# Sliding-window attention and a two-layer network on one core: score blocks of 64 queries by 128 keys, row sums from ones beside the values, chunks of 256 queries

## The chip, the cores and the metric

The kernel runs on one core of a Trainium2 chip. The metric is the time of one launch on the device in microseconds (us). The core has engines with a queue of instructions each, executed in the queue's order: PE multiplies matrices (PEld is its loading of weights), DVE and POOL work on vectors, ACT applies functions and copies, SP issues most of the transfers (DMA). PE writes to PSUM, which has eight banks; POOL does not read PSUM in this kernel.

## What is computed

For batch 8, 8 heads, 576 positions and head size 64 the reference does this (shortened):

```python
scores = scale * np.matmul(q, k.transpose(0, 1, 3, 2))
mask = np.abs(pos[:, None] - pos[None, :]) <= 32
scores = np.where(mask, scores, -1000000000.0)
attn = np.exp(scores - np.max(scores, axis=-1, keepdims=True))
attn = attn / (np.sum(attn, axis=-1, keepdims=True) + 1e-09)
x = np.matmul(attn, v)                  # heads side by side: 4608 tokens x 512
h = x @ w_in                            # 512 x 2048
out = np.maximum(0.01 * h, h) @ w_out   # 2048 x 512
```

A query meets at most 65 keys, those up to 32 positions away.

## The kernel before

**Units.** Attention is cut into units of one pair of heads (four pairs, one on partitions 0 to 63 and one on 64 to 127 of each tile) and one half of a batch's 576 queries, 288 of them: 64 units. `score` (L270) multiplies blocks of 64 keys with the queries that can reach them. The keys of a pair lie in `kbd` as blocks of 128 by 128 with one head in each diagonal quarter and zeros elsewhere, so one matmul does both heads. Five matmuls of 128, 128, 128, 96 and 64 columns make a unit's scores in the PSUM tile `ps`. ACT takes the exponential (L280, 576 columns), POOL multiplies with the mask (L282, `prob`). `product` (L312) multiplies `prob` with the values `vbd`, which are laid out in diagonal quarters too, in five matmuls. `sums` (L295) gets the row sums, broadcast to 64 partitions each, with a matmul by a block-diagonal matrix of ones (L301 on the two halves of `prob` that DVE has added in `join`, L292, from unit 12 on; L304 twice without that). DVE takes the reciprocal of the sums out of PSUM (L309) and multiplies (L334, `scaled`) into `xT`, the transposed input of the network.

**Network.** `h_tile` and `h_first` (L360, L369) make the first layer for one half of a batch, 288 tokens: 16 tiles `f` of four matmuls over the contraction (L348), each evicted by ACT with the leaky function (L355) into `gT`. `h_first` goes over the contraction outermost for four tiles, so that pass `c` needs only the units of pair `c`. `o_tile` (L381) makes 128 tokens of output by 16 matmuls of 512 columns (L390); ACT copies them out (L395, four buffers `o_sb`) and SP writes them. Four PSUM banks (`mm`) serve both layers.

**Inputs.** `load_qk` and `load_v` (L68, L87) fetch f32 data through SP's queue. POOL, and in the opening DVE and ACT, cast them to bf16 (L195, L197, L203, L205). Queries and keys of the first two batches are transposed on PE (`transposes`, L218) and copied out by ACT; later batches are transposed by a DMA (`transpose_dma`, L207). DVE copies the keys into the quarters of `kbd` (`place_keys`, L258, L260). From batch 2 on a packet of q or k has 512 bytes, as two rows go to one partition together.

**Order.** The program order is written by hand and every engine follows it. Lines 454 to 568 are the opening: batch 0 and its first layer, with `keep_busy` (L398), 21 matmuls whose result nobody uses, between them. POOL issues the loads of the weights (L448, L452), and a one-element memset on POOL (L75) holds back the loads of batch 1. In the opening a cast of batch 1 on DVE stands one or two pairs ahead of its transposes (`second_pair`, L546). From L574 a plan lists the network's work with its costs, and `spend` (L595) calls `step` (L420) whenever a unit is due: it issues `score(i + 2)`, then unit i's sums, product and scaling, then the casts, transposes and loads due at that step. Units for one half batch are due evenly over the network's work on the half before, and end 4 us ahead of it (`LEAD`).

Of the kernel before, what the change touches and what calls it, by code (L numbers as in the profile page):

```python
# [16 lines left out]
def kernel(  # L17
# [13 lines left out]

    nc = tc.nc
# [8 lines left out]
    NB = S // 64  # L41
    HALF = S // 2
    DMC = DMODEL // 128
    FFC = DFF // 128
    EVEN = HALF // 2
# [5 lines left out]
    cast = ctx.enter_context(tc.tile_pool(name="cast", bufs=1))  # L51
    attn = ctx.enter_context(tc.tile_pool(name="attn", bufs=2))
    kt = ctx.enter_context(tc.tile_pool(name="kt", bufs=4))
    joined = ctx.enter_context(tc.tile_pool(name="joined", bufs=2))
    recip = ctx.enter_context(tc.tile_pool(name="recip", bufs=3))
    outp = ctx.enter_context(tc.tile_pool(name="outp", bufs=4))
    PS = bass.MemoryType.PSUM
    mmps = ctx.enter_context(tc.tile_pool(name="mmps", bufs=4, space=PS))
    scps = ctx.enter_context(tc.tile_pool(name="scps", bufs=1, space=PS))
    xps = ctx.enter_context(tc.tile_pool(name="xps", bufs=1, space=PS))  # L60


    qf, kf, vf = {}, {}, {}
    RUN = S // 96

    BY_DMA = 2

    def load_qk(b, p, behind=None):  # L68

        for into, src, name in ((qf, q, "qf"), (kf, k, "kf")):
            t = fload.tile([96, 2, RUN * D], FP32, name=f"{name}{p}")
# [3 lines left out]
            heads = src[b, 2 * p:2 * p + 2]  # L77
            if b < BY_DMA:
                nc.sync.dma_start(out=t, in_=heads.rearrange("a (p c) d -> p a (c d)", c=RUN))
            else:  # L80
                nc.sync.dma_start(
                    out=t.rearrange("p a (g e) -> p a g e", g=3),
                    in_=heads.rearrange("a (g p c) d -> p a g (c d)", g=3, c=2),
                )
            into[b, p] = t

    def load_v(b, p):  # L87

        t = fload.tile([128, NB, D], FP32, name=f"vf{p}")
        for a in range(2):  # L90
            nc.sync.dma_start(
                out=t[64 * a:64 * a + 64],
                in_=v[b, 2 * p + a].rearrange("(c p) d -> p c d", p=64),
            )
        vf[b, p] = t

    load_qk(0, 0)
    load_qk(0, 1)
    load_v(0, 0)
    load_qk(0, 2)  # L100
    load_qk(0, 3)
    for p in range(1, NPAIR):
        load_v(0, p)

# [6 lines left out]
    ones_bd = const.tile([128, 128], BF16)  # L111
    nc.vector.memset(ones_bd, 0.0)
    nc.vector.memset(ones_bd[0:64, 0:64], 1.0)
    nc.vector.memset(ones_bd[64:128, 64:128], 1.0)

# [3 lines left out]

    kbd = [const.tile([128, NPAIR, NB, 128], BF16, name=f"kbd{i}") for i in range(2)]  # L120
    vbd = [const.tile([128, NPAIR, NB, 128], BF16, name=f"vbd{i}") for i in range(2)]
    zero = const.tile([128, 1], BF16)
    nc.vector.memset(zero, 0.0)

    def clear(t, p):
        flat = t[:, p].rearrange("p n j -> p (n j)")
        nc.scalar.activation(
            out=flat, in_=zero.to_broadcast([128, NB * 128]), func=AF.Copy,
        )

    mask = [const.tile([128, 2, 2, EVEN], BF16, name=f"mask{i}") for i in range(2)]
    nc.vector.memset(mask[0][:, 1, :, 0:16], 0.0)
    nc.vector.memset(mask[1][:, 1, :, 128:EVEN], 0.0)
    nc.vector.memset(kbd[0], 0.0)  # L134
    clear(vbd[0], 0)
    clear(vbd[0], 1)
    clear(vbd[0], 2)

    WIN = [
        [((0, 0, 48), (2, 48, 64), (4, 112, 32)), ((1, 16, 64), (3, 80, 64))],
        [((4, 0, 32), (6, 32, 64), (8, 96, 48)), ((5, 0, 64), (7, 64, 64))],
    ]

    win = const.tile([128, 2, 3, 64], BF16)
    nc.gpsimd.memset(win, 1.0)
    for lo in (0, 64):
        w = win[lo:lo + 64]
        nc.gpsimd.affine_select(  # L150
            out=w, in_=w, compare_op=ALU.is_ge, fill=0.0,
            base=0, channel_multiplier=-1, pattern=[[1, 2], [0, 3], [2, 64]],
        )
        nc.gpsimd.affine_select(
            out=w, in_=w, compare_op=ALU.is_ge, fill=0.0,
            base=2 * W, channel_multiplier=1, pattern=[[-1, 2], [0, 3], [-2, 64]],
        )
    nc.gpsimd.memset(vbd[0][:, 3], 0.0)
    win_f = win.rearrange("p c m i -> p c (m i)")

    def make_mask(hf):
        lo = (16, 32)[hf]
        nc.gpsimd.tensor_copy(out=mask[hf][:, 0], in_=win_f[:, :, lo:lo + EVEN])
        lo = (16, 0)[hf]
        nc.gpsimd.tensor_copy(out=mask[hf][:, 1, :, lo:lo + 128], in_=win_f[:, :, 0:128])

    NPROB = 6
    prob = const.tile([128, NPROB, 2, 2, EVEN], BF16)

    ps = scps.tile([128, 1024], FP32)  # L170
    P0 = 512 - HALF
    ps_v = ps[:, P0:P0 + 2 * HALF].rearrange("p (n c i) -> p n c i", n=2, c=2)
    nc.scalar.activation(
        out=ps[:, 512:512 + HALF], in_=zero.to_broadcast([128, HALF]), func=AF.Copy,
    )


    RING = 4 * HALF
    xT = const.tile([128, NPAIR, RING], BF16)
    w_in_bf = const.tile([128, DMC, DFF], BF16)  # L180
    w_out_bf = const.tile([128, FFC, DMODEL], BF16)


    qT = {}

    def cast_qk(b, p, q_eng=None):
        for eng, src, dst in ((q_eng or nc.gpsimd, qf, qb), (nc.gpsimd, kf, kb)):
            if b < BY_DMA:
                parts = [(dst[:, p], src[b, p].rearrange("p a (c d) -> p c a d", d=D))]
            else:  # L190
                by_c = src[b, p].rearrange("p a (g c d) -> c p g a d", g=3, c=2)
                parts = [(dst[:, p, 3 * c:3 * c + 3], by_c[c]) for c in range(2)]
            for to, tok in parts:
                if eng is nc.scalar:
                    eng.activation(out=to, in_=tok, func=AF.Copy)  # L195
                else:
                    eng.tensor_copy(out=to, in_=tok)  # L197

    def cast_v(b, p, on_act=False, heads=range(2)):
        for a in heads:  # L200
            r = slice(64 * a, 64 * a + 64)
            if on_act:
                nc.scalar.activation(out=vbd[b % 2][r, p, :, r], in_=vf[b, p][r], func=AF.Copy)  # L203
            else:
                nc.gpsimd.tensor_copy(out=vbd[b % 2][r, p, :, r], in_=vf[b, p][r])  # L205

    def transpose_dma(b, p):  # L207
        if b not in qT:
            qT[b] = attn.tile([128, NPAIR, S], BF16, name="qT")
        kT = kt.tile([128, S], BF16, name="kT")  # L210
        for t, src in ((qT[b][:, p], qb), (kT, kb)):
            nc.sync.dma_start_transpose(
                out=t.rearrange("p (c i) -> p c i", c=RUN),
                in_=src[:, p].rearrange("p c a d -> p (c a d)"),
            )
        landing.append((8 * (b - 1) + 4 + p, b, p, kT))

    def transposes(b):  # L218

        qT[b] = attn.tile([128, NPAIR, S], BF16, name="qT")  # L220
        for p in range(NPAIR):
            for which, src in (("q", qb), ("k", kb)):
                tp = mmps.tile([128, RUN, 96], BF16, name="tp", tag="mm")
                for c in range(RUN):
                    nc.tensor.transpose(  # L225
                        tp[:, c],
                        src[:, p, c].rearrange("p a d -> p (a d)"),
                        ident[0:96, 0:96],
                    )

                tok = tp.rearrange("p (e c) i -> p c i e", c=2)
                if which == "q":
                    nc.scalar.activation(
                        out=qT[b][:, p].rearrange("p (c i e) -> p c i e", c=2, e=RUN // 2),
                        in_=tok, func=AF.Copy,
                    )
                else:
                    kT = kt.tile([128, S], BF16, name="kT")
                    nc.scalar.activation(  # L239
                        out=kT.rearrange("p (i c) -> p i c", c=RUN),  # L240
                        in_=tp.rearrange("p c i -> p i c"), func=AF.Copy,
                    )
                    unplaced.append((b, p, kT))
                yield

    unplaced, landing = [], []

    def place_keys():

        while landing and landing[0][0] <= state["done"]:  # L250
            unplaced.append(landing.pop(0)[1:])
        while unplaced:
            b, p, kT = unplaced.pop(0)
            for a in range(2):
                r = slice(64 * a, 64 * a + 64)
# [394 lines left out]
```

## Time and profile before

| what | value |
|---|---|
| median of 3 runs | 320.66 us (320.07 to 321.24) |
| profiled execution, first to last instruction (span) | 319.0 us |
| what the median has beyond the span | 1.66 us |
| busy: PE, DVE, POOL, ACT | 301.1, 220.7, 191.2, 183.5 us |
| instructions: PE, DVE, POOL, ACT | 2429, 258, 251, 394 |
| granted PE clock | 1.00 throughout |
| DMA | 108,400 packets, 49.46 MB, queue of SP 66.0% of 16 engines |
| last matmul's end | 315.9 us |

For the profiled execution nothing but its span is known; its own launch time is taken to be the span and 1.66 us around it. A group line of the profile names line, engine, operation and tiles, then shapes and count; after the bar stand busy time and the mean length of one in ns, then the engine's idle time just before them and what ended it. Matmuls overlap, so a matmul's mean length is more than what it adds: that is read from the distance between starts.

### The profile page before, as it was taken

To read this page: it belongs to the slowest core of one execution; us is meant where nothing else is said; L and a number is where in the kernel's file an instruction comes from. 1 tells how busy PE (TensorE), PEld (TensorE's weight loads), DVE (VectorE), ACT (ScalarE), POOL (GpSimd) and SP (SyncE) were. 2 spreads that over 40 slices of the span, in tenths; PEclk is the share of its full clock that TensorE was granted. 3 is DMA by queue.
4 is the path that set the end of the run, shared out by engine and by line. 5 is a ranking of instruction groups with operands and counts; after the bars stand their busy time and mean duration, and the time that the engine had idled before them with its cause. 6 is when DMAs were issued, how large, how long until landed. Compare 5 with 4: busy or idle time off the path is not lost.

```text
span 319.0 us, 6455 instructions
## 1 busy us (share of the span) xinstructions
PE 301.1 (94%) x2429; PEld 203.5 (64%) x2449; DVE 220.7 (69%) x258; ACT 183.5 (58%) x394; POOL 191.2 (60%) x251
## 2 busy tenths in 40 slices
PE   2678998999999999999999999999999999999996
PEld 1457764576765858576765858576665858576653
DVE  5688886869755987688755987688745988565100
ACT  7686688574652828375552828465552837464531
POOL 7899963974646866585646866586637866330000
PEclk9999999999999999999999999999999999999999
DMA  8999998997998989399835996399833440000102
GB/s 189 224 184 229 269 242 188 242 200 180 223 245 167 245 148 210 79 237 202 173 76 114 233 229 151 74 215 223 178 76 104 108 71 33 35 35 2 66 31 71
DMA packets 108400, 49.46 MB, mean 155 GB/s; under 512 B 68816, under 2 KB 103888, under 8 KB 108368
## 3 DMA queue, kind: packets, MB, share of 16 engines
q1 hardware_dynamic: 104144, 44.84, 66.0%
q0 software_dynamic: 4224, 4.19, 8.1%
q8 instruction: 19, 0.31, 0.5%
q14 instruction: 13, 0.11, 0.1%
HBM read 36.70 MB, written 9.44 MB: 145 GB/s over the span
## 4 chain that ended last, share of the span: by engine, by line
PE 88%; DVE 5%; ACT 3%; issue 2%; POOL 1%; ACTq 0%; POOLq 0%; DVEq 0%
PE mm L390 38%; PE mm L348 37%; PE x L320 5%; PE ps L275 5%; PE s L301 2%; DVE r L309 2%; DVE qb L197 1%; PE s L304 1%; DVE kbd L258 1%; POOL prob L282 1%; ACT kT L239 1%; PE tp L225 1%; ACT e L280 1%; ACT vbd L203 1%; DVE kbd L134 1%
## 5 line engine op out<-in xcount | busy, mean ns | idle before, releaser
L309 DVE RECIPROCAL r<-s 128x288 f32<-128x288 f32 x64 | 125.2, 1956 | 57.0 <-PE s L301 53.3
L282 POOL TENSOR_TENSOR prob<-e,mask 128x576 bf16<-128x576 bf16 x64 | 81.6, 1276 | 89.2 <-ACT e L280 42.1
L348 PE MATMUL mm<-xT,w_in_bf 128*128 128x288 bf16 x1024 | 134.0, 286 | 0.1
L390 PE MATMUL mm<-w_out_bf,gT 128*128 128x512 bf16 (+2 forms) x572 | 128.7, 373 | 1.1
L355 ACT ACTIVATE gT<-mm 128x288 bf16<-128x288 f32 x256 | 101.2, 412 | 25.6 <-PE mm L348 9.1
L348 PEld LDWEIGHTS <-w_in_bf 128*128 128x128 bf16 x1024 | 98.4, 98 | 24.5 <-issue 0.3
L390 PEld LDWEIGHTS <-gT 128*128 128x128 bf16 x592 | 56.3, 98 | 59.2
L395 ACT ACTIVATE o_sb<-mm 128x512 f32<-128x512 f32 (+2 forms) x37 | 21.7, 585 | 91.8 <-PE mm L390 89.0
L280 ACT ACTIVATE e<-ps 128x576 bf16<-128x576 f32 x64 | 41.5, 648 | 10.6 <-PE ps L275 10.5
L197 POOL CAST kb<-kf 96x384 bf16<-96x384 f32 (+1 forms) x56 | 34.8, 643 | 4.5 <-DMA kf<-in_k_dram 4.3
L205 POOL CAST vbd<-vf 64x576 bf16<-64x576 f32 x50 | 34.7, 694 | 1.5
L334 DVE TENSOR_TENSOR xT<-x,r 128x288 bf16<-128x288 f32 x64 | 29.2, 457 | 7.8 <-PE x L320 1.1
L260 DVE COPY kbd<-kT 64x576 bf16<-64x576 bf16 x48 | 32.3, 674 | 0.6 <-DMA kT<-kb 0.3
L320 PE MATMUL x<-prob,vbd 128*128 128x128 bf16 (+2 forms) x320 | 26.0, 213 | 2.7 <-ACT vbd L203 1.3
L275 PEld LDWEIGHTS <-kbd 128*128 128x128 bf16 x320 | 20.8, 99 | 10.7 <-DVE kbd L258 1.6
L275 PE MATMUL ps<-qT,kbd 128*128 128x128 bf16 (+2 forms) x320 | 26.3, 214 | 1.3 <-DVE kbd L258 0.8
L197 POOL CAST qb<-qf 96x384 bf16<-96x384 f32 x48 | 24.4, 536 | 0.0
L320 PEld LDWEIGHTS <-vbd 128*128 128x128 bf16 x320 | 20.5, 99 | 5.4 <-ACT vbd L203 1.9
L292 DVE TENSOR_TENSOR both<-prob 128x288 bf16<-128x288 bf16 x52 | 20.0, 384 | 0.9
L301 PE MATMUL s<-both,ones_bd 128*128 128x288 bf16 x52 | 14.9, 286 | 0.0
L258 DVE COPY kbd<-kT 64x576 bf16<-64x576 bf16 x16 | 7.1, 446 | 6.2 <-ACT kT L239 6.0
L225 PE MATMUL tp<-ident,qb 96*128 96x96 bf16 x48 | 4.1, 233 | 6.8 <-DVE qb L197 6.8
(43 smaller groups left out, 87.9 us busy)
## 6 DMA issues: line engine op xcount, KB each, us to landing
qf<-in_q_dram SPq DMA_DIRECT2D x32, 288.0 KB, 4.6
kf<-in_k_dram SPq DMA_DIRECT2D x32, 288.0 KB, 5.3
vf<-in_v_dram SPq DMA_DIRECT2D x64, 144.0 KB, 4.4
out_dram<-o_sb SPq DMA_DIRECT2D x35, 256.0 KB, 3.9
w_in_bf<-in_moe_w_in_dram POOLq DMA_DIRECT2D x4, 512.0 KB, 8.2
w_out_bf<-in_moe_w_out_dram POOLq DMA_DIRECT2D x4, 512.0 KB, 16.4
qT<-qb SPq DMA_TRANSPOSE x24, 4.2
kT<-kb SPq DMA_TRANSPOSE x24, 3.1
```

The source lines that it names most:

```text
L197: eng.tensor_copy(out=to, in_=tok)
L205: nc.gpsimd.tensor_copy(out=vbd[b % 2][r, p, :, r], in_=vf[b, p][r])
L260: nc.vector.tensor_copy(out=to.rearrange("p n (m c) -> p n c m", c=2), in_=kT[r].rearrange("p (c n m) -> p n c m", c=2, n=NB),)
L275: nc.tensor.matmul(ps_v[:, n_, :, i0:i0 + n], kbd[b % 2][:, p, blk], by_c[:, :, hf * EVEN + i0:hf * EVEN + i0 + n], start=True, stop=True,)
L280: nc.scalar.activation(out=e, in_=ps[:, P0:P0 + 2 * HALF], func=AF.Exp, scale=scale)
L282: nc.gpsimd.tensor_mul(pr.rearrange("p n c i -> p (n c i)"), e, mask[hf].rearrange("p n c i -> p (n c i)"),)
L309: nc.vector.reciprocal(r, s)
L320: nc.tensor.matmul(x_v[:, :, i0:i0 + n], vbd[b % 2][:, p, blk, :], pr[:, n_, :, i0:i0 + n], start=(blk == parts[0][1]), stop=(blk == parts ...
L334: nc.vector.tensor_mul(place(i), x, r)
L348: nc.tensor.matmul(h[:, 0:HALF], w_in_bf[:, c, ts(f, 128)], xT[:, c, ds(g * HALF % RING, HALF)], start=(c == 0), stop=(c == DMC - 1),)
L355: nc.scalar.activation(out=gT[:, f, ds(g * HALF % RING, HALF)].rearrange("p (i c) -> p i c", c=2), in_=h[:, 0:HALF].rearrange("p (c i) -> ...
L390: nc.tensor.matmul(o[:, lo:hi], gT[:, f, ds(128 * j % RING, 128)], w_out_bf[:, f, lo:hi], start=(f == 0), stop=(f == FFC - 1),)
```

## The change

The work is tiled anew. A unit is one pair of heads and 256 queries, counted through the 4608 tokens without regard to batches: 18 chunks, 72 units. A unit has four windows of 64 queries, and each window meets 128 keys, from 32 before to 32 behind. The keys lie plainly in `kz` with 32 zero columns at either end; the queries in `qz` are padded, each head with zeros in the other head's 64 partitions. One matmul of 128 columns does a window's scores for both heads. The values lie in `vw` as head 0, ones, head 1, so that a 128-wide weight holds one head's values and ones, and each product brings its row sums on the other 64 partitions: eight matmuls of 64 columns a unit. ACT then copies the sums across to the value's partitions (two copies of 64 by 256), DVE takes the reciprocal from SBUF and multiplies twice on 64 partitions.

The first layer takes 256 tokens for the first four chunks and 512 from then on. `sums`, `join`, `keep_busy`, `kbd` and `place_keys` go; the DMA transposes the keys straight into `kz`, and DVE copies the transposed queries into `qz` (`place_queries`, two contiguous copies per pair). PSUM has two banks for scores and two for `x`, which the opening's transposes share; before, `ps` was one tile over two banks, and `x` and `s` had one bank each. Output buffers go from four to three. One row goes to a partition in loads of q and k from batch 2 on, so packets have 256 bytes. The values are loaded in blocks of 128 rows shifted by 32.

```diff
+    CH = 256
     def score(i):
+        ps = scps.tile([128, 2, CH // 64, 64], FP32, name="ps")
+        for w, (b, m) in enumerate(windows(i)):
+            nc.tensor.matmul(
+                ps[:, :, w], kz[b % 2][:, p, 64 * m:64 * m + 128],
+                qz[b % 2][:, p, :, 64 * m:64 * m + 64], start=True, stop=True,
+            )
...
+        nc.gpsimd.tensor_mul(pr.rearrange("p a w i -> p (a w i)"), e, mask)
     def product(i):
+        for a in range(2):
+            for w, (b, m) in enumerate(windows(i)):
+                nc.tensor.matmul(
+                    x[:, a, w],
+                    vw[b % 2][:, p, m, a:a + 2].rearrange("p n d -> p (n d)"),
+                    pr[:, a, w], start=True, stop=True,
+                )
+        x = x.rearrange("p a w i -> p a (w i)")
+        s = norm.tile([128, CH], FP32, name="s")
+        nc.scalar.activation(out=s[0:64], in_=x[64:128, 0], func=AF.Copy)
+        nc.scalar.activation(out=s[64:128], in_=x[0:64, 1], func=AF.Copy)
+        r = norm.tile([128, CH], FP32, name="r")
         nc.vector.reciprocal(r, s)
+        for a in range(2):
+            rows = slice(64 * a, 64 * a + 64)
+            nc.vector.tensor_mul(xT[rows, p, t0:t0 + CH], x[rows, a], r[rows])
```

`transpose_pe` transposes a pair's queries and keys on PE, for batch 1 a half of the rows at a time, and copies out with ACT (queries of head 0, then keys) and DVE (queries of head 1). The opening is written anew. In it a `part` of batch 1 casts and transposes at once:

```diff
+    def part(p, hf, tag=None):
+
+        cast("q", 1, p, nc.vector, hf)
+        cast("k", 1, p, nc.gpsimd, hf)
+        transpose_pe(1, p, hf, tag)
...
+    cast("q", 0, 2, nc.scalar)
+    product(0)
+    load_w_in(0, 512)
+    transpose_pe(0, 2)
+    first_v(1)
+    score(2)
+    product(1)
...
     for f in range(4, FFC):
+        h_tile(0, CH, f)
+        if f in (5, 8, 11):
             second_half()
+            p = state["done"] - NPAIR
+            cast_v(0, p, 4, WPB, nc.gpsimd, nc.gpsimd, nc.gpsimd)
+            load_w_out(p)
...
+    o_part(1, (0, 1))
+    step()
+    cast_v(1, 2, 0, 3, nc.gpsimd, nc.gpsimd, nc.gpsimd)
+    load_v(1, 2, (1,))
+    part(0, 1, True)
+    load_qk(2, 0)
+    o_part(1, (2, 3))
+    step()
+    cast_v(1, 3, 0, 3, nc.gpsimd, nc.gpsimd, nc.gpsimd)
+    load_v(1, 3, (1,))
+    part(1, 1, True)
+    load_qk(2, 1)
+    o_part(2, (0, 1))
+    o_part(2, (2,))
...
+    step()
+    part(2, 1, True)
...
+    step()
+    part(3, 1, True)
```

Here `first_v` and `cast_v` cast the values (even windows in one instruction on 128 partitions, odd ones in two of 64), and `o_part(n, js)` does a quarter of the 16 matmuls of the output tiles `js`, of which four are open at once in the four `mm` banks. In the loop of 16 first-layer tiles shown, `h_tile(0, CH, f)` is the first layer of chunk 0. The plan's segments, its weights and its dues are new too:

```diff
+    segments = [[2], [3]] + [[c, c + 1] for c in range(4, NCH, 2)]
+    LEAD, H_W, O_W = 5.0, 0.8, 1.2
...
+    due = []
+    for g in range(1, len(segments)):
+        n = NPAIR * len(segments[g])
+        prev = at[g - 1] - (LEAD if g > 1 else 0.0)
+        due += [prev + (at[g] - LEAD - prev) * (i + 1) / n for i in range(n)]
```

`step` still issues `score(i + 2)`, then unit i's product with its copies, reciprocal and multiplications, then the query copies, casts, transposes and loads due; from batch 2 on the casts of a pair of q and k and those of v are all on POOL, as before.

More of the change, by code (lines that the diff above doesn't have):

```diff
@@ L109 @@
     nc.vector.tensor_copy(out=ident, in_=ident_f)
[L111 to L114, printed above, removed]
+    one = const.tile([128, 1], BF16)
+    nc.vector.memset(one, 1.0)
     qb = const.tile([96, NPAIR, RUN, 2, D], BF16)
     kb = const.tile([96, NPAIR, RUN, 2, D], BF16)
-    kbd = [const.tile([128, NPAIR, NB, 128], BF16, name=f"kbd{i}") for i in range(2)]
-    vbd = [const.tile([128, NPAIR, NB, 128], BF16, name=f"vbd{i}") for i in range(2)]
@@ L122 @@
[L122 to L135, printed above, removed]
@@ L158 @@
[L158 to L172, printed above, removed]
@@ L179 @@
+    for n in range(2 * CH // D):
+        nc.gpsimd.tensor_copy(out=mask[:, ts(n, D)], in_=mask1)
+    clear_k(0, nc.gpsimd)
+    clear_edges(0, nc.gpsimd)
+    RING = 4 * CH
     xT = const.tile([128, NPAIR, RING], BF16)
+    gT = const.tile([128, FFC, RING], BF16)
     w_in_bf = const.tile([128, DMC, DFF], BF16)
     w_out_bf = const.tile([128, FFC, DMODEL], BF16)
[L184 to L205, printed above, removed]
+    def copy(eng, out, in_):
+        if eng is nc.scalar:
+            eng.activation(out=out, in_=in_, func=AF.Copy)
+        else:
+            eng.tensor_copy(out=out, in_=in_)
@@ L575, with o_part @@
-    plan = []
-    tiles = 0
-    for g in range(1, 2 * B):
-        if g > 1:
-            plan += [(H_US, "h", g, f) for f in range(FFC)]
-        while 128 * (tiles + 1) <= HALF * (g + 1):
-            plan += [(O_US, "o", tiles, i) for i in range(4)]
+    os_ = [bank() for _ in range(4)]
+    def o_part(n, js):
+        for j in js:
+            o_mms(j, os_[j], range(4 * n, 4 * n + 4))
+    o_part(0, (0, 1))
+    part(2, 0, True)
+    score(9)
+    o_part(0, (2, 3))
+    cast_v(1, 1, 0, 3, nc.gpsimd, nc.gpsimd, nc.gpsimd)
@@ L582 @@
+    LEAD, H_W, O_W = 5.0, 0.8, 1.2
+    plan, tiles = [], 4
+    for g, seg in enumerate(segments):
+        n = CH * len(seg)
+        plan += [(H_W * DMC * (n * US + 2.5e-3), "h", g, f) for f in range(FFC)]
+        while 128 * (tiles + 1) <= CH * (seg[-1] + 1):
+            plan += [(O_W * 4 * 0.216, "o", tiles, i) for i in range(4)]
             tiles += 1
```

564 lines of the change are left out of this document (257 added, 307 removed).

## The prediction

> **What bounds the kernel now.** I read the busy tenths over the span first, then sums by stage, then matmuls in order of time, then the costly groups, and last the opening. In the tenths, PE is full from the fourth slice on.
>
> ```profile
> PE   2678998999999999999999999999999999999996
> DVE  5688886869755987688755987688745988565100
> POOL 7899963974646866585646866586637866330000
> ```
>
> The stages say it in us (length, then busy time of PE, PEld, DVE, ACT and POOL):
>
> ```profile
> 0.00:26.60 26.60, 14.95 (x151) 11.36 (x152) 17.97 (x27) 19.51 (x29) 22.70 (x36) 1.00 1.11 199
> 61.40:297.60 236.20, 235.35 (x1859) 157.89 (x1875) 174.78 (x205) 127.78 (x288) 143.65 (x190) 1.00 0.71 148
> ```
>
> From 61.4 us on PE is busy 99.6%, while DVE has 74%. There only PE's work counts. In the first 26.6 us PE is half idle and POOL has 85%: there the order counts. What a matmul adds is the distance between starts:
>
> ```profile
> 149.35 0.59 PE L390 MATMUL mm<-w_out_bf,gT 128*128 128x512 bf16 x2
> 149.79 0.40 PE L275 MATMUL ps<-qT,kbd 128*128 128x96 bf16 x5
> 150.03 0.29 PE L301 MATMUL s<-both,ones_bd 128*128 128x288 bf16 x1
> 150.15 0.40 PE L320 MATMUL x<-prob,vbd 128*128 128x64 bf16 x5
> 150.39 0.38 PE L390 MATMUL mm<-w_out_bf,gT 128*128 128x512 bf16 x1
> ```
>
> Two of 512 columns take 0.44 (the trace has 216 ns each), a unit's five score matmuls, 544 columns, 0.24, its sums 0.12. All fit columns / 2.4 ns plus 2.3 ns: 109 ns for 256 columns, 122.5 for 288, 56 for 128, 28.4 for 64, although each has its own weights.
>
> **PE's work.** Before: first layer 1024 x 0.1225 = 125.4 us, second 124.3 (560 full, the last tile in two widths), scores and products 64 x 0.24 = 15.4 each, sums 52 + 24 = 76 x 0.1225 = 9.3, transposes 96 x 0.043 = 4.1: 293.9. So 25.1 of the 319.0 us are lost: about 18.9 until the first layer's last pass over the contraction starts (25.8 us), some 3 from there to 61.4, 3.1 after the last matmul. After: first layer 256 x 0.109 + 448 x 0.2158 = 124.6, second 124.3, scores 288 x 0.056 = 16.1, products 576 x 0.0284 = 16.4, no sums, transposes 4.1: 285.5. The change takes **8.4 us** off PE. The one row missing is eight matmuls of 64 columns in succession: not under 28.4 ns by the rows, not over the 56 of a 128-column one, which would add 15.9. I take 28.4, since single ones run at that here with a new weight each.
>
> [...]
>
> **What a unit costs the others.** Rows:
>
> ```profile
> L309 DVE RECIPROCAL r<-s 128x288 f32<-128x288 f32 x64 | 125.2, 1956 | 57.0 <-PE s L301 53.3
> L282 POOL TENSOR_TENSOR prob<-e,mask 128x576 bf16<-128x576 bf16 x64 | 81.6, 1276 | 89.2 <-ACT e L280 42.1
> L395 ACT ACTIVATE o_sb<-mm 128x512 f32<-128x512 f32 (+2 forms) x37 | 21.7, 585 | 91.8 <-PE mm L390 89.0
> L205 POOL CAST vbd<-vf 64x576 bf16<-64x576 f32 x50 | 34.7, 694 | 1.5
> L334 DVE TENSOR_TENSOR xT<-x,r 128x288 bf16<-128x288 f32 x64 | 29.2, 457 | 7.8 <-PE x L320 1.1
> ```
>
> By length in columns: reciprocal 256 / 288 x 1.956 = 1.74, two multiplications of 0.42, so DVE has 2.58 us a unit. ACT: exponential 0.60 as the 512-column copy, sum copies 0.38 each (its forms of 512 and 128 columns, 597 and 277 ns, give the slope). Mask 512 / 576 x 1.276 = 1.14. From a product's end to its last multiplication: 0.57 (rest of the next exponential, ahead in ACT's queue) + 0.76 + 1.74 + 0.84 = 3.9 us. Before, the reciprocal ran beside the product, and one multiplication followed. In later stages this is covered: eight units per 512 tokens are 20.6 us of DVE and, with casts, some 23 of POOL beside 31.2 of PE, and the last unit has four quarters of an output tile (3.5 us) and six matmuls (1.3) before its result is needed, 4.8 against 3.9. That is 0 here; with 1 us more in the chain, each of eight segments would lose 0.1 or more.
>
> DMA: 27,648 packets more of the same bytes in all. At the mean of SP's queue (66.0% x 16 x 319 us over 104,144, 32 ns) that is at most 55 us of share, 0 if bytes count. DMA stands at 0.71 after 61.4 us, inputs come a batch ahead: I take 0. The third output buffer's absence is covered by 3.5 us between output tiles and 3.9 to land; SP's waits decide, also 0.
>
> **The opening, followed by hand in program order.** (a) Batch 0. Transposes of pair 2 and 3 leave PSUM partly through DVE, behind a whole unit there: product 0 ends at about 11.5, unit 0 leaves DVE at 15.9, the copy at 16.5, `score(2)` follows; unit 1 leaves at 21.0, `score(3)` at 21.6. POOL, with the masks, value casts (0.7 a pair), key casts (0.85) and weight issues (0.8) in line, gives the last value cast at 25.3; product 3 and its 3.9 us end at 29.1. The last pass starts there, not at 25.8, with 5.6 us of work done, not 6.9: 23.5 lost. Bounds: as now (18.9) and 3 more.
>
> (b) Chunks 0 and 1, 14.7 us of PE. DVE has units 4 to 7 one by one, from 33.3 (product 4, its exponential and copies behind evictions) to 43.9, and chunk 1's last pass waits for that. Then POOL clears the second buffers (2 x 2.1, ones 2.2, rest 0.6, from memsets of 1.06 us for 1152) and casts keys at 47.5, with PE there at 46.1. End at 51.9: 8.1 lost, 1.7 of it as `keep_busy` is gone. Without a cover PE starts slow:
>
> ```profile
> 12.94 0.69 PE L225 MATMUL tp<-ident,qb 96*128 96x96 bf16 x6
> 13.42 0.68 PE L225 MATMUL tp<-ident,kb 96*128 96x96 bf16 x6
> ...
> 39.06 0.42 PE L225 MATMUL tp<-ident,qb 96*128 96x96 bf16 x6
> 39.32 0.42 PE L225 MATMUL tp<-ident,kb 96*128 96x96 bf16 x6
> 45.07 0.43 PE L225 MATMUL tp<-ident,qb 96*128 96x96 bf16 x6 [0.66 <-DVE qb L197]
> ```
>
> Six transposes take 0.48 early and 0.26 later, though the granted clock reads 1.00. The last line is the wait to watch: PE for DVE's cast.
>
> (c) Output tiles 0 to 3, 17.6 us of PE with units, **the largest term**. After each of `step` 8 to 11 a `part` follows at once. Its query cast stands on DVE behind the unit just produced, its transposes on PE ahead of the next output matmuls: PE stands idle for 3.9 + cast 0.45 (half of the 96x768 cast, 0.64 to 1.6) + hand-over 0.1 = 4.5 us, four times: 18.0. POOL's key cast behind the mask of `score(i + 2)` and a value cast comes at 0.8 + 1.14 + 0.85 + 0.5 = 3.3, earlier. `part(3, 0)` waits 1.7 for POOL after `score(9)`. In all 19.7 lost.
>
> (d) Segment of chunk 3: 17.5 us of PE (7.0 + 6.9 + 8 x 0.45), but eight units are due in it, for the first segment of 512. DVE needs 8 x 2.58 and five pairs' query copies of 0.7 (from the 0.67 of the strided ones; half if contiguity helps), 24.1; POOL in steps 14 to 21 has eight masks of 1.14, five casts of a pair of q and k (2 x 0.88, the 96x768 casts take 0.82 to 0.93) and four of v (columns 640 and twice 512 at the 694 ns of 576, 2.0), less the last cast, 24.2. With two `x` banks PE can't run ahead: 6 lost (3 to 7).
>
> Sum: 285.5 + 23.5 + 8.1 + 19.7 + 6 + 1 for joints + 3.1 at the end = 346.9 of span, against 319.0. With 1.66 between span and median: **348.6 us**.
>
> **Rivals.** (1) *The clock falls in the gaps.* For: after an idle opening PE ran at half rate until 14 us. Against: no gap after 20 us in this trace is over 1.5 us. After each stall of 4.5 us about 2.2 us of work follow; at half rate that is up to 2.2 more, four times: 349 to 358, 355 taken. [...] (2) *Small products run at the cost of 128 columns*: 364.5. Against: the 28.4 ns. (3) *Half the waits*: casts or DVE's part shorter than taken, 2.5 us a stall, chunk 3 losing 3, the opening 3 better: 331. (4) *Not slower: PE's work alone decides*, as after 61.4 us now. If each `part` finds its cast done when PE arrives, so that the queue's order costs nothing and loss stays at 25.1, the span is 310.6 and the time 312.3. It decides once total loss is under 33.5 us; DVE's own order speaks against it, since the cast stands behind the unit in the same queue, and PE's order puts the transposes ahead of every other matmul at that place.
>
> **How the numbers follow.** Forecast (338 to 354) 0.50, rival (1) 0.16, (2) 0.06, (3) 0.20, (4) 0.08. Its own range with rivals (1) and (3) makes 0.86 between 326 and 360, some 0.8 when the edges of these are let go; that is the range. A difference of 0.3% is about what a measurement can tell from none. Faster 0.07 and same 0.01 from (4), slower 0.92.
>
> **What would show it.** PE's tenths down to 3 to 6 between 50 and 90 us, with four waits of 4 to 5 us of transposes for DVE's cast; first dense pass at 29, chunk 1's last pass at 44, output from 52, chunk 2's first layer near 89 us; a loss of about 6 us one segment later, with DVE full; PE at over 99% after; product starts 28 ns apart. It is wrong if those waits are short, if PE has gaps in the segments of 512, or if products stand 50 ns apart.

## The result and the profile after

The changed kernel takes 378.86 us (median of 4 runs, 378.24 to 380.51) beside 320.37 us of the kernel before (4 runs): 1.1835 times as long, 95% interval 1.1801 to 1.1869. The profiled execution spans 377.4 us, against 319.0. The forecast was 348.6, with a range of 326 to 360. Where the time went is read by stages, from the starts of matmuls in order of time:

| stretch | forecast | measured |
|---|---|---|
| start to chunk 0's last pass | 29.1 | 32.3 |
| to the first output matmul | 22.8 | 26.3 |
| output tiles 0 to 3, to chunk 2's first layer | 37.4 | 49.3 |
| chunks 2 and 3, to the first segment of 512 tokens | 39.2 | 51.2 |
| from there to the end | 218.4 | 218.2 |

The busy tenths of the changed kernel's page, with the granted clock:

```profile
PE   1448676555497478899999999999999999999996
DVE  4453832333307679975786776777678676576000
POOL 8566965243526679862476875886687673230000
PEclk9999989758679789999999999999999999999999
```

PE stands at 9 from slice 18 on, where before it stood at 8 or 9 from the fourth, and the clock row has holes in the output stage (slices 8 to 12) and behind it in chunk 2's segment. The stages (length, busy time of PE, PEld, DVE, ACT, POOL, then granted clock, DMA share, GB/s):

```profile
0.00:26.60 26.60, 9.67 (x96) 7.85 (x96) 12.54 (x17) 16.49 (x30) 17.98 (x40) 1.00 0.87 172
61.40:297.60 236.20, 202.04 (x1470) 109.48 (x1467) 155.11 (x210) 139.51 (x299) 147.47 (x189) 0.93 0.86 155
58.60:108.00 49.40, 28.07 (x155) 13.66 (x154) 15.89 (x23) 13.62 (x32) 19.92 (x35) 0.72 0.58 115
...
191.00:374.00 183.00, 183.00 (x1243) 93.24 (x1242) 114.08 (x153) 119.47 (x238) 95.31 (x114) 1.00 0.62 118
```

The same 236 us that were 99.6% PE before have 34 us of idle PE now, 21 of them in the output stage of 49.4 us, where no other engine is busy even half of the time: an order, not an amount. From 191 us on nothing is lost. The matmuls of that stage show the order:

```profile
66.03 0.30 PE L227 MATMUL tp<-ident,kb 96*128 96x96 bf16 x3 [2.66 <-POOL kb L193]
66.17 3.11 PE L340 MATMUL mm<-w_out_bf,gT 128*128 128x512 bf16 x8
...
74.57 0.42 PE L227 MATMUL tp<-ident,qb 96*128 96x96 bf16 x3 [4.44 <-DVE qb L193]
74.79 0.44 PE L227 MATMUL tp<-ident,kb 96*128 96x96 bf16 x3
75.03 3.61 PE L340 MATMUL mm<-w_out_bf,gT 128*128 128x512 bf16 x8
...
102.71 0.42 PE L227 MATMUL tp<-ident,qb 96*128 96x96 bf16 x3 [4.78 <-DVE qb L193]
```

Four waits of transposes for DVE's cast (4.44, 4.46, 4.64, 4.78 us) stand where the prediction put them. Behind each, and behind POOL's 2.66, matmuls run at half rate for some 3 to 5 us: eight output matmuls take 2.9 to 3.4 us, up to the start of what follows, and not 1.73, and twelve 3.9 to 4.8, not 2.6. Over the stage the slow matmuls stand some 9.5 us further apart than columns / 2.4 ns plus 2.3 ns. In chunk 2's segment PE waits for DVE's query copies, 9.2 us in four waits:

```profile
119.55 0.27 PE L273 MATMUL ps<-qz,kz 128*128 128x128 bf16 x2 [1.55 <-DVE qz L258]
...
125.51 0.37 PE L273 MATMUL ps<-qz,kz 128*128 128x128 bf16 x2 [3.62 <-DVE qz L258]
...
130.80 0.27 PE L273 MATMUL ps<-qz,kz 128*128 128x128 bf16 x2 [2.58 <-DVE qz L258]
```

Three more in chunk 3's segment make 3.3. Seven units stand in chunk 2's segment and six in chunk 3's. What the prediction took from rows of the kernel before is seen in the costly groups and, for the small products, in a settled stretch:

```profile
L300 DVE RECIPROCAL r<-s 128x256 f32<-128x256 f32 x72 | 126.2, 1753 | 92.2 <-ACT s L298 91.2
L281 POOL TENSOR_TENSOR pr<-e,mask 128x512 bf16<-128x512 bf16 x72 | 83.0, 1153 | 119.0 <-ACT e L278 114.6
...
L304 DVE TENSOR_TENSOR xT<-x,r 64x256 bf16<-64x256 f32 x144 | 60.8, 422 | 8.5
```
```profile
224.84 0.39 PE L273 MATMUL ps<-qz,kz 128*128 128x128 bf16 x4
225.07 0.40 PE L290 MATMUL x<-pr,vw 128*128 128x64 bf16 x8
225.30 4.48 PE L308 MATMUL mm<-xT,w_in_bf 128*128 128x512 bf16 x20
```

Four scores take 0.23 us and eight products 0.23, so 29 ns each.

### The profile page after: what moved, and what is told of

The parts are those of the page before. It is cut to its first block, busy times and chain, and to the rows that moved or that the text cites. A ratio compares the mean times of both kernels' runs of the same rounds, so it can differ in the third digit from the quotient of the medians.

```text
span 377.4 us, 6485 instructions
## 1 busy us (share of the span) xinstructions
PE 313.8 (83%) x2256; PEld 174.4 (46%) x2256; DVE 219.6 (58%) x290; ACT 217.4 (58%) x464; POOL 209.1 (55%) x290
## 4 chain that ended last, share of the span: by engine, by line
PE 68%; DVE 12%; POOL 6%; ACT 6%; DMA 4%; issue 3%; SPq 0%; DVEq 0%; POOLq 0%; ACTq 0%
PE mm L340 31%; PE mm L308 28%; DVE r L300 6%; PE ps L273 4%; PE x L290 3%; DVE xT L304 3%; DMA kf<-in_k_dram 2%; ACT e L278 2%; POOL vw L193 2%; DVE qz L258 2%; POOL pr L281 1%; DMA qt<-qb 1%; ACT s L297 1%; ACT s L298 1%; PE tp L227 1%
## 5 line engine op out<-in xcount | busy, mean ns | idle before, releaser
L300 DVE RECIPROCAL r<-s 128x256 f32<-128x256 f32 x72 | 126.2, 1753 | 92.2 <-ACT s L298 91.2
L281 POOL TENSOR_TENSOR pr<-e,mask 128x512 bf16<-128x512 bf16 x72 | 83.0, 1153 | 119.0 <-ACT e L278 114.6
L308 PE MATMUL mm<-xT,w_in_bf 128*128 128x512 bf16 (+1 forms) x704 | 137.2, 349 | 5.1 <-DVE xT L304 4.2
L314 ACT ACTIVATE gT<-mm 128x512 bf16<-128x512 f32 (+1 forms) x176 | 84.8, 521 | 23.8 <-PE mm L308 21.8
L278 ACT ACTIVATE e<-ps 128x512 bf16<-128x512 f32 x72 | 42.9, 596 | 52.7 <-PE ps L273 52.6
L193 POOL CAST vw<-vf 64x512 bf16<-64x512 f32 (+6 forms) x116 | 64.9, 559 | 6.5 <-DMA vf<-in_v_dram 1.9
L304 DVE TENSOR_TENSOR xT<-x,r 64x256 bf16<-64x256 f32 x144 | 60.8, 422 | 8.5
L273 PE MATMUL ps<-qz,kz 128*128 128x128 bf16 x288 | 31.7, 232 | 18.8 <-DVE qz L258 12.5
L290 PE MATMUL x<-pr,vw 128*128 128x64 bf16 x576 | 31.3, 199 | 4.4 <-POOL vw L193 4.4
L297 ACT ACTIVATE s<-x 64x256 f32<-64x256 f32 x72 | 27.4, 381 | 6.0 <-PE x L290 4.2
L298 ACT ACTIVATE s<-x 64x256 f32<-64x256 f32 x72 | 27.1, 376 | 0.8
L193 POOL CAST qb<-qf 96x768 bf16<-96x768 f32 x24 | 19.8, 826 | 0.0
```

The costliest lines, as they stand in the source:

```text
L193: eng.tensor_copy(out=out, in_=in_)
L273: nc.tensor.matmul(ps[:, :, w], kz[b % 2][:, p, 64 * m:64 * m + 128], qz[b % 2][:, p, :, 64 * m:64 * m + 64], start=True, stop=True,)
L278: nc.scalar.activation(out=e, in_=ps.rearrange("p a w i -> p (a w i)"), func=AF.Exp, scale=scale)
L281: nc.gpsimd.tensor_mul(pr.rearrange("p a w i -> p (a w i)"), e, mask)
L290: nc.tensor.matmul(x[:, a, w], vw[b % 2][:, p, m, a:a + 2].rearrange("p n d -> p (n d)"), pr[:, a, w], start=True, stop=True,)
L297: nc.scalar.activation(out=s[0:64], in_=x[64:128, 0], func=AF.Copy)
```

## Experiments

Times are of single runs, with the span of the profiled execution (after: 377.4), unless a ratio is given. In kernels with added lines the line numbers are a few off.

### The output stage

**e1.** Casts of batch 1's second half a step earlier, ahead of the unit on DVE:

```diff
+    part_cast(0, 1)
     o_part(1, (0, 1))
     step()
-    part(0, 1, True)
+    transpose_pe(1, 0, 1, True)
+    part_cast(1, 1)
```

> Against the changed kernel's span of 377.4 us. Only the place of the casts of batch 1's second half is moved: each stands one step earlier on DVE and POOL. Theory (queue order: the transposes on PE wait for a cast that stands on DVE behind the unit just produced): the four waits of 4.4 to 4.8 us shrink to 1 to 2.5 us, since product 9 still waits for the bank of unit 8; the stretch from the first output tiles (58.6) to the first layer of chunk 2 (108.0) shortens by 4 x 2.5 to 3.5 = 10 to 14 us, and by up to 8 more if PE then stays at its full rate: span 356 to 367. Rival (the queries' or keys' transfers or the two shared banks of x hold the transposes): the waits keep their length with another name beside them, span above 374.

364.3 us, span 362.5. The output stage falls from 49.3 to 29.5 us; of its four waits 0.47 us at most is left, and PE waits for a bank of `x` and, in the next stage, for an output copy instead:

```profile
75.51 0.39 PE L290 MATMUL x<-pr,vw 128*128 128x64 bf16 x8 [1.94 <-DVE xT L304]
...
92.17 2.89 PE L308 MATMUL mm<-xT,w_in_bf 128*128 128x256 bf16 x25 [2.33 <-ACT o_sb L347]
```

So the place of the cast in DVE's queue made the waits. Of the 19.8 us won here 4.9 are lost elsewhere: chunks 2 and 3 take 54.9 us instead of 51.2, and the output began 1.2 us later.

**e3.** Idle matmuls in the waits, nothing else changed (24 before `part(3, 0)`, 44 before each later `part`):

```diff
+    keep_busy(44)
     part(0, 1, True)
```

> The order stays; 24 and four times 44 matmuls of 224 columns whose result nobody uses are put where PE waits for the casts between 63 and 103 us (4.2 us each if PE runs at its full rate). Theory (PE falls to half its rate after each of these gaps): the waits stay, but the eight output matmuls behind each go from 2.9 to 3.5 us back to 1.73, the twelve from 4.0 to 4.8 to 2.6, and scores and products with them: 7 to 10 us less, span 367 to 371. Rival (the slow matmuls have another cause, such as the output tiles' weights or a busy memory): no change, span 376 to 379, and if the fillers themselves run at half rate up to 8 us more.

372.39 us, span 370.6. The waits are as long as before, with the fillers in them; the matmuls behind them run at full rate again (7 in 1.51 us), and the stage takes 40.2 us instead of 49.3:

```profile
69.79 4.38 PE L492 MATMUL busy<-mask,ident 128*128 128x224 bf16 x44
74.59 0.30 PE L227 MATMUL tp<-ident,qb 96*128 96x96 bf16 x3 [0.42 <-DVE qb L193]
...
75.08 1.67 PE L340 MATMUL mm<-w_out_bf,gT 128*128 128x512 bf16 x7
```

The half rate behind the waits cost 9.1 us by this pair of runs, close to the 9.5 added up in the trace after, and an idle PE was its cause.

### The opening

**e6.** Batch 0's second-head query copy leaves PSUM through ACT, not DVE:

```diff
-        copy(nc.vector, at(qz[b % 2][64:128, p, 1, t0:t0 + nt]), tq[64:128])
+        copy(nc.scalar if b == 0 else nc.vector,
```

> Only batch 0's transposed queries of the second head leave PSUM through ACT instead of DVE. Theory (score 2 and score 3 wait for a copy that stands on DVE behind units 0 and 1, 3.1 and 1.4 us): each of both comes 1 to 1.5 us earlier, the last pass of chunk 0 starts at 29 to 30.5 instead of 32.3, and all behind it as much earlier: span 374 to 376. Rival (POOL's line of masks, casts and weight issues sets it): under 0.7 us, span above 376.5.

381.47 us, span 379.7: a miss. Chunk 0's last pass comes at 31.8, 0.5 earlier, as the rival had it. The score now waits for ACT's key copies (1.65 and 1.59 us) and product 3 for POOL's value cast (1.48). The output stage, with its instructions unchanged, took 51.5 us here instead of 49.3. Over the kernels that leave these instructions alone it takes 47.7 (e10) to 51.6 us, with 21 to 22 us of waits in each: the half rate begins and ends at other matmuls. Against these bounds e3's gain is 7.5 to 11.3 us. Differences of 2 us of span between single runs are therefore read stage by stage here.

**e11.** Value casts of pairs 1 and 2 moved into POOL's idle time before the loop:

```diff
+    cast_v(0, 1, 4, WPB, nc.gpsimd, nc.gpsimd, nc.gpsimd)
+    cast_v(0, 2, 4, WPB, nc.gpsimd, nc.gpsimd, nc.gpsimd)
```

> Only POOL's casts of the later values of pairs 1 and 2 of batch 0 are moved to where POOL idles (33.3 to 36.2 us). Theory (DVE's four units in line set chunk 1's last pass): products 5 and 6 no longer wait for values, but the last pass of chunk 1 comes only 0.8 to 1.5 us earlier than 48.8, since DVE is busy from 37.0 on for four units of 2.6. Rival (POOL's line sets it): 2.5 to 3.5 us earlier. The hold on batch 1's loads, at 45.0, is released 2 to 3 us earlier in both.

377.86 us, span 376.1. Chunk 1's last pass comes at 47.9 instead of 48.8, the output 1.9 us earlier.

### Chunks 2 and 3: order

From here on D is the stretch from chunk 2's first layer to the first segment of 512 tokens (51.2 us after), S that segment (31.8).

**e4.** All segments of 256 tokens:

```diff
-    segments = [[2], [3]] + [[c, c + 1] for c in range(4, NCH, 2)]
+    segments = [[c] for c in range(2, NCH)]
```

> The first layer takes 256 tokens throughout, so no segment has eight units due within 17.5 us of PE's work. Theory of the forecast (the bunch of eight units in chunk 3 costs 6 us): the waits at units 22 to 24 (3.3 us) go and those at units 16 and 17 shrink, 5 to 8 us less there; the first layer's 448 matmuls of 512 columns become 896 of 256, 1 us more, and ACT has 19 us more of evictions, hidden where PE has 3.9 us a unit: span 370 to 374. Rival (the placing of queries alone is the cause): under 2 us less there, span 376 to 380. If ACT becomes the bound in the first layer, more than 380.

374.23 us, span 372.4. D is 41.4, a gain of 9.8, and what follows it is 4.1 longer, so that 5.7 are left. D has 9 units there and not 13, so 1.8 us of the gain is PE's own work that moved behind it. Eight units due ahead of one segment of 512 were a real cost; four remain.

**e2.** `place_queries()` before `product(i)`:

> Only DVE's copies of the transposed queries are moved, ahead of the unit of the same step instead of behind it. Theory (new since the result: score i + 2 waits on PE for copies that stand on DVE behind unit i - 1's reciprocal and multiplications, 1.55 + 3.6 + 2.6 + 1.4 us at units 14 to 17 and 3.3 at 22 to 24): these waits go, and the stretch from chunk 2's first layer (108.0) to the first segment of 512 (159.2) shortens from 51.2 by 8 to 12 us, to 39 to 43, which is what the forecast had from the amounts of work on DVE and POOL: span 365 to 369. Rival (amounts of work alone: eight units in 17.5 us): under 3 us, span above 374. If the transposing transfers land too late, DVE waits for them instead, and the gain is under 5.

385.53 us, span 383.7: a miss, and slower. D is 52.4. The copies now stand in DVE's queue ahead of the unit and wait for the transposing transfer, with the unit behind them:

```profile
DVE qz L258 <- DMA qt<-qb: 12.7, 12, 2.1
```

**e5.** The query copies on ACT:

```diff
-                nc.vector.tensor_copy(out=qz[b % 2][r, p, a], in_=t[r])
+                nc.scalar.activation(out=qz[b % 2][r, p, a], in_=t[r], func=AF.Copy)
```

> Against the changed kernel's 51.2 us from chunk 2's first layer to the first segment of 512, 33.2 of them PE's own work. The copies of the transposed queries go from DVE to ACT, at the same place in the order. Theory A (the score waits for copies that stand on DVE behind a unit's 2.6 us, and the copies take DVE's time too): the seven waits of 0.5 to 3.6 us shrink by some 1.5 to 2 us each, the stretch takes 40 to 44 us, span 366 to 371. Theory B (amounts: eight units bunched, 20.6 us of DVE and 24 of POOL in 17.5): DVE has 5 us less to do but POOL is unchanged, the stretch takes 46 to 49, span 372 to 376. If ACT stalls on a transfer that has not landed, evictions wait and segments of 512 lose time: the last 218 us grow.

384.43 us, span 382.6: a miss. D is 48.0, as theory B had it, and chunk 2's segment takes 22.9 us instead of 29.7, but ACT waits 10.2 us in all for the transposing transfers, with PE's evictions behind it, and five segments of 512 take 32.7 to 33.4 us instead of 31.3 to 31.8.

**e10.** Casts, transposes and copies due one step earlier:

```diff
-            qk_due.setdefault(base(b) - (5 if b == 2 else 6) + p, []).append((b, p))
+            qk_due.setdefault(base(b) - (6 if b == 2 else 7) + p, []).append((b, p))
```

> The changed kernel with only the earlier dues of the run before, segments of 512 left. Theory of the order: the four waits at units 14 to 17 (9.2 us) go, the three at 22 to 24 (3.3) too, and the slow matmuls between; the stretch from chunk 2's first layer to the first segment of 512 falls from 51.2 to 38 to 42, near the forecast's 39.2. Theory of amounts: DVE and POOL have 24 us of work in 17.5 of PE's in chunk 3, the stretch stays above 45 and the waits change their names (PE for DVE's xT or POOL's values).

376.31 us, span 374.6. D is 46.7, which the theory of amounts had above 45, but S is 35.7: together 82.4 against 83.0. The waits for query copies shrink to 1.4 to 2.3 us, and waits for a free `x` bank come in their place. All 16 query copies of D and S run beside POOL's work now, 10 of 16 did before, and they take 11.6 us instead of 8.0. DVE has no gap from 110.7 to 151.3 us:

```profile
110.70:151.30 40.60, 29.39 (x285) 19.76 (x282) 38.70 (x47) 24.27 (x62) 33.86 (x42) 1.00 1.04 179
```

### Together

**e7** has the edits of e1, e4, e5 and e6 and the first 24 fillers; **e8** those of e1 and e4 and the 24 fillers; **e9** is e8 with the dues of e10.

> All repairs in one: casts one step earlier, 24 filling matmuls before the last first-half part, chunks of 256 throughout, query copies on ACT, batch 0's copies out of PSUM on ACT. If the terms add (15 for the casts, 1.6 for the clock there, 5 net for the chunks, 3 to 5 for the copies on ACT beside them, 2 for batch 0): span 348 to 352. If they hide one another: 353 to 360. The kernel before, with 319.0, stays ahead in either case, since chunks 0 and 1 and the first output tiles still lose over 25 us.

371.72 us, span 369.9: a miss. ACT waits for transfers (9.2 us in four waits), PE for ACT, and five of the later chunks take 18.5 to 19.0 us instead of 15.85.

> The three repairs that each shortened their own stretch, together, without the two moves to ACT: casts one step earlier, 24 filling matmuls, chunks of 256 throughout. By stretches: 58.5 to the first output tiles as now, 29.4 for these (as with all repairs), 41.4 to the first layer of chunk 4 (as with chunks of 256), 222.3 after (the same): span 350 to 354. If the query copies on ACT were not what cost the version with all repairs its 18 us, span 362 to 370.

356.22 us (median of 4 runs), 1.1126 times the kernel before (1.1092 to 1.1159). The output stage takes 27.9 us (29.4 expected), D 45.0 (41.4 expected). It is the fastest variant, and still slower than the kernel before.

> As the run before, and from batch 2 on the casts of q and k, their transposes and DVE's query copies come due one step earlier. Theory (the first of three limits in chunks 2 and 3 is that the copies are due only one unit before the score that reads them, with DVE one unit behind): the 41.4 us from chunk 2's first layer to chunk 4's become 36 to 38, against 33.2 of PE's work, span 346 to 350. Rival (amounts of POOL's and DVE's work, or the transposing transfers, which follow POOL's casts by 5 to 6 us): over 40 us there, no gain in the span.

357.51 us, span 355.8: a miss. D is 41.9, but a wait of 4.03 us for an output copy is new in it, as ACT waits 4.08 us for one of the three output buffers to be written out, and the segments after it take 16 to 20.

### Chunks 2 and 3: amounts

Here work is taken away. e12 is e10 with 128 of 256 columns in the reciprocal. From batch 2 on, e13 (from e12) and e14 (from e10) leave out the value casts, e15 (from e13) also the loads of values from batch 3 on; e16 (from the changed kernel) and e17 (from e12) load q and k in packets of 1536 bytes, with the tokens in another order.

```diff
-            cast_v(b, p, 0, WPB, nc.gpsimd, nc.gpsimd, nc.gpsimd)
...
-                    out=t.rearrange("p a (c d) -> p a c d", d=D),
-                    in_=heads.rearrange("a (c p) d -> p a c d", p=96),
+                    out=t, in_=heads.rearrange("a (p c) d -> p a (c d)", c=RUN))
```

> The kernel with the earlier dues (e10_earlier_dues, 374.6 us of span) with one difference: the reciprocal covers 128 of a unit's 256 columns, and the multiplications use these twice, so that half of the reciprocals are left out of the computation. DVE's part of a unit falls from 2.61 to about 1.75 us (a reciprocal of 1.75 becomes 0.88), nothing else is less. Theory of amounts: over chunks 2 and 3 and the first segment of 512 tokens DVE is the bound, as it ran without a gap from 110.7 to 151.3 us there, so the stretch from chunk 2's first layer to the end of that segment falls from 82.4 us by about 13 units x 0.87 = 11, less where PE's own work is reached: 71 to 74. Chunk 1's last pass stands behind four units one by one and comes 0.87 x 4 = 3.5 earlier, less what POOL's line takes back: 45.4 to 46.5. The four waits of transposes for DVE's cast in the output stage fall from 4.5 to 4.8 by 0.87 each, to some 3.9. Span 355 to 361. Rival: the stretch is bound by POOL's casts and masks (some 25 us), by the transposing transfers, or by the order of the queues; then it stays over 79 us, and the span over 367.

> As e12_half_reciprocal (half of the reciprocals left out), and POOL's casts of the values are left out from batch 2 on, which takes 2.06 us a pair off POOL, some 12 us of the stretch from chunk 2's first layer to the end of the first segment of 512 tokens (83.9 us in e12, of which PE's own work is 62.6). Theory: DVE and POOL are two bounds of nearly equal size, and the stretch moves only when both are relieved: 66 to 74 us, and a span of 353 to 362. Rival: SP's queue, which issues without a gap there, or the order of the queues: over 79 us, and a span over 366.

> As e10_earlier_dues (82.4 us from chunk 2's first layer to the end of the first segment of 512 tokens, span 374.6), with POOL's casts of the values left out from batch 2 on; all reciprocals are there. Theory of two bounds: DVE's 13 units of 2.61 us and its query copies still hold the stretch, except that the copies run faster when POOL is idle beside them (0.30 instead of 0.67 to 0.95 us, 16 copies, some 6 us at most): 76 to 81 us, and a span of 368 to 374. Rival one: POOL alone is the bound, then it falls as far as in e13. Rival two, SP or order: no change within 2 us.

> As e13_no_value_casts, with the loads of the values left out too from batch 3 on: SP's queue issues four transfers a pair less, some 1.9 us, about 15 us over the stretch. Theory of DVE and POOL: 0 to 4 us less than e13. Rival, SP's queue is the bound: the stretch falls by 8 us or more against e13, to some 66 to 72.

> The changed kernel with one difference: from batch 2 on the loads of q and k take six rows of 64 in a run to one partition, 1536 bytes, instead of one row of 256. Bytes, issues and all instructions are the same, 960 packets fewer of 1152 in each of these 48 loads; the tokens come in another order, so that attention is computed for permuted queries and keys. Theory of packets: the stretch from chunk 2's first layer to the end of the first segment of 512 tokens (83.0 us) is paced by some 640 packets per us; some 12 of these loads fall in it, 11,500 packets, worth up to 18 us, of which DVE's amount (38.7 of 40.6 us busy in e10) lets go 3 to 7: 76 to 80 us, and a span of 370 to 374; the score's waits for query copies get shorter than 9.2 us, and the transposing transfers land earlier. Rival: the share of the DMA engines is a queue that nobody waits for, so that the stretch stays within 2 us of 83.0 and the span over 375.

> As e12_half_reciprocal (casts due a step earlier, half of the reciprocals left out; 83.9 us from chunk 2's first layer to the end of the first segment of 512 tokens, span 370.9), with the same longer packets as in e16_long_packets, so q and k come permuted. Theory of packets: with DVE and the DMA engines both relieved the stretch falls more than by either alone: 70 to 77 us, and a span of 357 to 364. Rival (POOL's order, SP's issues, which are the same as in e12): it stays over 81, and the span over 368.

| kernel | relieved | D + S | span |
|---|---|---|---|
| after | | 51.2 + 31.8 = 83.0 | 377.4 |
| e16 | packets | 51.7 + 31.5 = 83.2 | 378.7 |
| e10 | order | 46.7 + 35.7 = 82.4 | 374.6 |
| e14 | order, POOL | 44.8 + 34.4 = 79.2 | 374.6 |
| e12 | order, DVE | 48.3 + 35.6 = 83.9 | 370.9 |
| e13 | order, DVE, POOL | 47.9 + 31.9 = 79.8 | 368.1 |
| e17 | order, DVE, packets | 43.6 + 32.9 = 76.5 | 366.8 |
| e15 | order, DVE, POOL, SP's loads | 40.7 + 33.5 = 74.2 | 363.2 |

For D and S, e12 and e13 fell to their rivals, and DVE's amount as the only bound fell with them; e14 came where its theory had it, and its 16 query copies take 7.4 us instead of e10's 11.6. e17's 76.5 is in its range, its span is not. Elsewhere e12 did what was expected or more: chunk 0's last pass at 30.0 (32.3 in e10), chunk 1's at 44.3 (48.8), the four waits 3.64 to 3.84 us. What stopped it in D is the transposing transfer. DVE's waits for it, in e12 and then in e17:

```profile
DVE qz L258 <- DMA qt<-qb: 11.8, 5, 5.4
```
```profile
DVE qz L255 <- DMA qt<-qb: 1.1, 2, 0.9
```

In e12 SP issues 55 transfers in 49 us with no gap over 0.11 us between them, among them transposes of 1.2 to 2.0 us each with waits for POOL's casts in them, and the share of the 16 DMA engines reads 102%, with 644 packets per us. Longer packets alone change nothing in the changed kernel (e16, its theory fell); with the casts due earlier and DVE relieved they are worth 7.4 us (e17, where the output stage was 2.4 us longer than in e12, so that the span shows less), and POOL's casts 4.1 (e13), and SP's loads 5.6 more (e15, between its two expectations). So there are two bounds close together: DVE's units and copies, and what brings the queries, POOL to SP to DMA. Half of the reciprocals alone win nothing (e12), POOL's casts alone 3.2 us (e14); the long packets were not tried with the earlier dues and all reciprocals. That DVE's bound stands first is argued from its row without a gap in e10, not shown. How SP's issues and the DMA engines share the other isn't settled, as e15 takes away both. PE's own work in D and S is 64.8 us by the row of the columns, with 21 units (the expectations' 62.6 is too low); the 9 us that e15 still has above it were not traced to one cause.

## Why the prediction was wrong in size

The kernel became slower, as forecast, and by the waits that were forecast, but the time is 30.3 us above the sum; the four stretches ahead of the first segment of 512 tokens hold all of it.

**Right.** PE's work: 29 ns for a small product (28.4 taken), and the last stretch at 218.2 us (218.4). Durations: 1.753 us for the reciprocal (1.74), 0.422 for a multiplication (0.42), 1.153 for the mask (1.14), 0.38 for a sum copy. The four waits, their names, places and lengths (4.5 taken, 4.44 to 4.78). That more packets cost nothing in this kernel: e16 bears it out. For the output buffer, three instead of four, no run tests it alone; the longest wait of an output copy for a transfer is 0.81 us here, and 4.08 in e9. Rivals (2), (3) and (4) fell: no 50 ns products, no shorter stalls, no cast done in time. Rival (3)'s 331 doesn't follow from the terms given: 2.5 us less in four stalls and 3 less in two places make 332.6; nothing hangs on it.

**Term (c), 11.9 us too small.** The step that failed is that the sum had the stalls alone, and the half rate behind them stood only as rival (1), "against: no gap after 20 us in this trace is over 1.5 us". That a trace has no long gap says nothing of what a long gap does; the rows of the opening, six transposes in 0.48 us and later in 0.26, spoke for the rival. e3 gives it 9.1 us, where the rival had at most 2.2 each, 8.8. So rival (1) had this mechanism and its size, but its 349 to 358 us is 21 us or more short, as the other terms in it stayed too small. The waits were 1.6 longer than taken (2.66 for 1.7 at `part(3, 0)`, the four 0.3 in all, 0.34 at another). By these two the stage is 48.1 of its 49.3. The trace after has half rate behind all four waits of 4.44 to 4.78 us, and behind the wait of 2.66 us too.

**Term (d), 12.0 too small.** The step that failed here: it counted DVE's and POOL's work of chunk 3's segment alone, with all eight units of chunks 4 and 5 in it, and gave chunk 2's segment nothing. The plan ends units 5 us ahead of their segment (`LEAD`), so three of the eight stand in chunk 2's segment. The trace has 9.2 us of waits there, 3.3 in chunk 3's segment and some 2.5 of half rate behind the longer ones; with PE's own 33.6 (13 units) that is 48.6 of 51.2. Where the step had a sum of amounts for one segment, the trace has a chain of four queues: the copy on DVE stands behind the unit, the transpose on SP behind POOL's cast, the cast behind the mask. e4 shows the part that the bunch of eight units has (9.8 us of D, 5.7 with what follows). A better order alone doesn't win the rest: e10 to e17 show that taking away one queue's work or delay brings out the next, and which share of the 12 us each queue has stays open.

**Terms (a) and (b), 3.2 and 3.5 too small.** In (a) POOL's eight copies that build the mask, which the prediction gives no price, take 3.0 us ahead of the first key cast at 7.2 (5.3 before). `score(2)` stands at 18.34 instead of 16.5, behind DVE's copy, and product 3 waits for the value cast:

```profile
18.34 0.59 PE L273 MATMUL ps<-qz,kz 128*128 128x128 bf16 x4 [3.08 <-DVE qz L193]
...
27.69 0.23 PE L290 MATMUL x<-pr,vw 128*128 128x64 bf16 x1 [1.51 <-POOL vw L193]
```

In (b) chunk 1's last pass stood 1.7 us later behind chunk 0's than forecast (16.5 for 14.8), and the output another 1.8: POOL cleared the second buffers from 45.1 to 52.3 us and cast batch 1's keys at 53.5, after 1.25 us of waiting for their load, and not at 47.5. e6 and e11 move single steps of it and win 0.5 and 0.9: several queues carry the chain in turn. e12 moves DVE's unit, and wins 2.3 and 4.5.

## What to carry to other kernels

A stall of PE is priced with the half rate behind it: here 21 us of waits, each of 2.7 to 4.8 us, cost 9 more. When a change puts a cast or copy on an in-order queue right behind a long unit, and its user on PE right after that unit, the whole unit is added to every pass; issue the cast a step earlier (19.8 us of the stage here, half rate included). Where four queues pass work on in a short stage, take no bound from one queue's sum: find the second bound before pricing the relief of the first.

## What the runs showed of the hardware

- Slow matmuls follow every wait of PE of 3.64 to 4.84 us in these runs, and shorter ones only sometimes. Of nine waits of 3.61 or 3.62 us two, in e3 and e8, had full rate behind them up to the next wait, and one, in e12, has another wait straight behind it. The 2.66 or 2.67 us ahead of a key transpose, in 14 runs, had slow output matmuls behind them in 11 (the changed kernel among them) and full rate in e10, e11 and e12; after 2.00 us in D of e12 the matmuls were slow. The granted clock reads 0.72 over the output stage, but 1.00 over the first 26.6 us, where six transposes take 0.46 to 0.49 us instead of 0.26.
- In the changed kernel the same DVE copy of 64 by 576 takes 0.30 us (median of 38 without POOL's work beside it) or 0.66 (median of 10 beside it, from 0.30 to 0.86). What makes the difference is not shown by these rows.
